# Linear attention and a low-rank mixer on one core: other zero products around q's transposes, the 1e-6 of the denominators added by PE, and v's first transfers moved between two casts

## The chip, the core and the metric

The kernel runs on one core of a Trainium2 chip. Its time is device time in microseconds. It is measured in several runs, and one further execution is recorded by the hardware profiler; that one gives the profile and the trace. The engines are named as in the profile: PE (matrix products; PEld is its weight load), DVE, ACT, POOL, and SP, which here only issues transfers. POOL issues transfers as well. All transfers are carried by the core's 16 DMA engines.

## What is computed

The reference works on q, k and v of 8 batches, 8 heads, 576 positions and 64 features, in fp32:

```python
c, s = cos(pi/2 * pos/576), sin(pi/2 * pos/576)
phi = lambda x: concat([relu(x) * c, relu(x) * s])       # 128 features
kv  = einsum('bhsf,bhsd->bhfd', phi(k), v)
den = einsum('bhsf,bhf->bhs', phi(q), phi(k).sum(2)) + 1e-6
x   = einsum('bhsf,bhfd->bhsd', phi(q), kv) / den        # heads side by side: 576 x 512 a batch
u   = x + (x.T @ U @ V).T                                # U: 576 x 32, V: 32 x 576
out = u + relu(u @ w1) @ w2                              # w1: 512 x 2048, w2: 2048 x 512
```

## The kernel before

**Tiling.** The 576 positions of a batch are cut into nines: row m of a tile holds positions of the nine m // 2, even rows the first five and odd rows the last four, so that a batch is four tiles of 128 rows (c = 0 to 3) and a tail of 64 rows (c = 4). Each of q, k and v has one staging tile (`qst`, `kst`, `vst`), which is filled by a load of the odd rows (`load_odd`, L94) and one of the even rows (`load_even`, L88). SP issues these loads in the order of the program, and a load for the next batch can only be issued when the staging tile's old content has been used.

**Order.** The schedule is written by hand: each engine executes its instructions in the order in which the program issues them. The program has an opening for batch 0 (L1176 to L1231), which is what the change touches, and then a list of slots, one group of PE products after another, with smaller work hung in between (`beside`, `todo`). In the slots, `g1_main` (L562) multiplies a 128-column piece j of w1 with the transposed u of a batch into a PSUM bank (`g_ps`, L572), and ACT applies the Relu and copies it into `hid` (L581). There are three such banks. In the first 16 slots (batch 0) hangs the attention of batch 1: its q features and transposes, then `k_prep` in slots 6, 7, 9, 10 and 12, one half on DVE (L304) and one on ACT (L302), starting with the tail `k_tl`.

**The opening.** A tile of zeros, `zero`, is made first by DVE (L140). SP issues the loads of q, of k and of the second half of v (heads 4 to 7); POOL issues the loads of V and U (`load_uv`, L165), fills constants, casts V to bf16 in three pieces (`cast_v`, L246), and only then issues the loads of v's first half (heads 0 to 3) into a tile `v0` of its own (`load_v0`, L155, issues at L156 and L160). These convert fp32 to bf16 on the way. Then POOL issues the first two quarters of w1 (`w1_load`, L115) and casts U.

PE meanwhile multiplies zeros with zeros into an unused bank (`keep_warm`, L225): `n` products of 512 columns and then `short` products of 128. Such products change no result. Then, for each c, ACT and DVE make q's features (`q_prep`) and PE transposes them, eight products of 128 columns each (`qtr_mm`, L371), with one long zero product after each group. Five copies out of PSUM (`qtr_evac`, L378: c = 0, 2, 4 by DVE, 1 and 3 by ACT) and four more long zero products follow. After that `spread_v` (L263) copies V onto all rows, and for each c the features of k are made (`k_prep`), their sums z taken (L1203), and k times v0 is summed in `kv0_mm` (L1098, the products at L1101): for c = 0 to 2 ahead of z's last round, and for the rest after it.

**first_chain** (L1113) casts the second half of v, copies z and kv out of PSUM, and computes the denominators of four heads at a time: `den_mm` (L1053) makes 20 products of one column each into a bank `d_ps`, `recip` (L407) adds 1e-6 on DVE into SBUF (L408) and takes the reciprocal there (L409). The numerators are multiplied by it (`xh_norm` by DVE, `xh_scale` by ACT), and the chain goes on to u, its transposes and the first products with w1 (L589). After `first_chain`, SP's loads of batch 1 (q, k, v) stand in the program; POOL issues the last two quarters of w1 once k's tail of batch 0 has been read (L1216), and w2 once k of batch 1 has landed (L1227).

Of the kernel before, what the change touches and what calls it, by code (L numbers as in the profile page):

```python
# [11 lines left out]
BF16 = mybir.dt.bfloat16  # L12
# [5 lines left out]
def kernel(  # L18
# [11 lines left out]
    nc = tc.nc  # L30
# [3 lines left out]
    S = 576  # L34
    D = 64
    E = D + 1
    P = 128
# [3 lines left out]
    NJ = DH // P  # L41
    NPAIR = B // 2
    TS = 64

    def tail(b):
        lo = TS * (b % 2)  # L50
# [3 lines left out]
    pool = ctx.enter_context(tc.tile_pool(name="work", bufs=2))  # L54
# [29 lines left out]
    def nines(src, b):  # L84
        return src[b].rearrange("h (m k) d -> m h (k d)", k=9)
# [41 lines left out]
    def cast(eng, o, i):  # L127
        if eng is nc.scalar:
            nc.scalar.activation(out=o, in_=i, func=AF.Copy, bias=0.0, scale=1.0)
        else:  # L130
            eng.tensor_copy(out=o, in_=i)  # L131


    V_, A_, G_ = nc.vector, nc.scalar, nc.gpsimd
# [20 lines left out]
    def load_v0():  # L155
        nc.gpsimd.dma_start(  # L156
            out=v0[1:P:2, :, 0:4].rearrange("m h c d -> m h (c d)"),
            in_=nines(v, 0)[:, 0:4, 5 * D : 9 * D],
        )
        nc.gpsimd.dma_start(  # L160
            out=v0[0:P:2].rearrange("m h c d -> m h (c d)"),
            in_=nines(v, 0)[:, 0:4, 0 : 5 * D],
        )

    def load_uv():  # L165
# [16 lines left out]
        out=iota[:, 0:4], pattern=[[2, 4]], base=0, channel_multiplier=9,  # L182
        allow_small_or_imprecise_dtypes=True,
    )
    for lo in (0, TS):
        nc.gpsimd.iota(
            out=iota[lo : lo + TS, 4:5], pattern=[[1, 1]], base=8, channel_multiplier=18,
# [3 lines left out]
        out=iota[:, 5:6], pattern=[[1, 1]], base=8, channel_multiplier=9,  # L191
# [6 lines left out]
        out=par, in_=ident[:, 1:P:2], op=ALU.add, axis=mybir.AxisListType.X  # L198
    )
    V_.tensor_scalar(  # L200
        out=iota[:, 0:4], in0=iota[:, 0:4], scalar1=par, scalar2=None, op0=ALU.add
# [19 lines left out]
    V_.memset(v_ext[:, 0:4, :, D:E], 1.0)  # L221
    V_.memset(q_tlT, 0.0)
    V_.memset(x_tl, 0.0)

    def keep_warm(n, tag, bufs, short=0):  # L225
        w_ps = ps.tile([P, 512], FP32, tag=tag, bufs=bufs, name="w_ps")
        for i in range(n + short):
            w = 512 if i < n else P
            nc.tensor.matmul(  # L229
                out=w_ps[:, 0:w], lhsT=zero[:, 0:P], rhs=zero[:, 0:w], start=True, stop=True  # L230
            )
# [6 lines left out]
    V_nat = pool.tile([R, S], BF16, tag="S2", bufs=2, name="V_nat")  # L238
# [4 lines left out]
        G_.memset(v_ext[:, 4 + i, :, :], 0.0)  # L243
        G_.memset(v_ext[tail(i), 4 + i, :, D:E], 1.0)

    def cast_v():  # L246
        nine_v = stV.rearrange("r (m k) -> r k m", k=9)
        for i in range(2):
            cast(
                G_,  # L250
                V_nat[:, 0:512].rearrange("r (c m i) -> r c m i", c=4, i=2)[:, :, :, i],
                nine_v[:, 5 * i : 5 * i + 4, :],
            )
        cast(G_, V_nat[:, 512:S], nine_v[:, 4, :])

    def cast_u():
        cast(G_, U_bf[:, 0:4, :], stU[:, 0:4, :])
# [14 lines left out]
    def spread_evac(eng):  # L272
        cast(eng, V_bf, v_ps[0].rearrange("r (c p) -> r c p", c=4))
        cast(eng, V_tl, v_ps[1][:, 0:TS])
# [5 lines left out]
    def v_prep(b, h0=0, h1=H, cs=range(5), engs=None):  # L280
        vx = v_ext
        for n, c in enumerate(cs):
            eng = engs[n] if engs else G_
            if eng is None:
                continue
            if c < 4:
                cast(eng, vx[:, c, h0:h1, 0:D], vst[:, h0:h1, c, :])
            elif b < 2:
                cast(eng, v_tl[:, h0:h1, 0:D], vst[:, h0:h1, 4, :])
            else:  # L290
                cast(eng, vx[tail(b), 4 + b % 2, h0:h1, 0:D], vst[tail(b), h0:h1, 4, :])

    def v_block(b, h0, h1, c0, c1, eng):
        cast(
            eng,
            v_ext[:, c0:c1, h0:h1, 0:D].rearrange("p c h d -> p h c d"),
            vst[:, h0:h1, c0:c1, :],
        )
# [98 lines left out]
    def qT_of(b, c, h):  # L397
        return q_pT[b][:, c, h, :] if c < 4 else q_tlT[:, h, :]
# [8 lines left out]
    def recip(rec, den):  # L407
        nc.vector.tensor_scalar(out=rec, in0=den, scalar1=1e-6, scalar2=None, op0=ALU.add)  # L408
        nc.vector.reciprocal(out=rec, in_=rec)  # L409
# [25 lines left out]
    def A_of(b):  # L435
        return A_sb[b % 4]
# [614 lines left out]
    O2, G3 = ("o", 2), ("g", 3)  # L1051

    def den_mm(b, h0, h1, d_ps):  # L1053
        for c in range(5):
            for h in range(h0, h1):
                nc.tensor.matmul(
                    out=d_ps[:, c, h - h0 : h - h0 + 1],
                    lhsT=qT_of(b, c, h),
                    rhs=z_sb[:, h : h + 1],
                    start=True,  # L1060
                    stop=True,
                )

    def xh_mm(b, c, h0, tag=None, bufs=None, acc=None):
# [41 lines left out]
    def xh_scale(b, c, h0, rec, acc):  # L1106
        for i in range(4):
            nc.scalar.activation(
                out=x_of(b, c)[:, (h0 + i) * D : (h0 + i + 1) * D], in_=acc[:, i, :],
                func=AF.Copy, bias=0.0, scale=rec[:, c, i : i + 1],  # L1110
            )

    def first_chain(b):  # L1113
        v_block(b, 4, 8, 3, 4, A_)
        v_prep(b, 4, 8, (4,), (A_,))
        v_block(b, 4, 8, 0, 3, V_)
        cast(A_, z_sb, z_ps)
        cast(V_, kv_sb[b][:, 0:4, 0:D], kv_lo)
        spread_evac(A_)
        d0 = ps.tile([P, 2, 512], FP32, tag="X", bufs=1, name="d_ps")  # L1120
        d = [d0[:, i, 0:20].rearrange("p (c h) -> p c h", h=4) for i in range(2)]
        rec = [pool.tile([P, 5, 4], FP32, tag="rec5", bufs=2, name="rec5") for _ in (0, 1)]
        den_mm(b, 0, 4, d[0])
        recip(rec[0], d[0])
        x0 = [xh_mm(b, c, 0, *G3) for c in ORD[0:3]]
        for n in (0, 1):
            xh_norm(b, ORD[n], 0, rec[0], x0[n])
        kv_unit(b, 1, *O2, A_, D)
        for c, tg in zip(ORD[3:], (O2, T1)):
            x0.append(xh_mm(b, c, 0, *tg))  # L1130
        den_mm(b, 4, 8, d[1])
        xh_scale(b, ORD[3], 0, rec[0], x0[3])
        xh_norm(b, ORD[2], 0, rec[0], x0[2])
        recip(rec[1], d[1])
        xh_norm(b, ORD[4], 0, rec[0], x0[4])
        x1 = [xh_mm(b, c, 4, *G3) for c in ORD[0:2]]
        a_ps = ps.tile([P, DM], FP32, tag="o", bufs=2, name="a_ps")
        for _ in range(2):
            nc.tensor.matmul(out=a_ps, lhsT=zero[:, 0:P], rhs=zero, start=True, stop=True)
        x1.append(xh_mm(b, ORD[2], 4, *G3))  # L1140
        x34 = ps.tile([P, 2, 512], FP32, tag="X", bufs=1, name="x34_ps")
        for i in range(2):
            x1.append(x34[:, i, 0:256].rearrange("p (i d) -> p i d", d=D))
            xh_mm(b, ORD[3 + i], 4, acc=x1[-1])
        A_mm(b, a_ps, (0, 1))
        xh_scale(b, ORD[2], 4, rec[1], x1[2])
        for n in (0, 1):
            xh_norm(b, ORD[n], 4, rec[1], x1[n])
        cast(V_, A_of(b)[0:TS, :], a_ps[0:TS, 0:P])
        uT_alloc(b)  # L1150
        for i, (tag, bufs) in enumerate((T1, O2)):
            uT_ps[b, i] = ps.tile([P, 4, P], FP32, tag=tag, bufs=bufs, name="uT_ps")
            open_mm(b, i, uT_ps[b, i], range(4))
        for i in range(2):
            uTd_mm(b, i)
        uTd_evac(b, 0, A_)
        for n in (3, 4):
            xh_norm(b, ORD[n], 4, rec[1], x1[n])
        uTd_evac(b, 1, V_)
        A_mm(b, a_ps, (2, 3))  # L1160
        cast(A_, A_of(b)[TS:P, :], a_ps[TS:P, 0:P])
        u2 = ps.tile([P, 2, 512], FP32, tag="X", bufs=1, name="u2")
        uT_ps[b, 2] = u2[:, 0, :].rearrange("p (c t) -> p c t", c=4)
        uT_ps[b, 3] = ps.tile([P, 4, P], FP32, tag="T", bufs=1, name="uT_ps")
        for i in (2, 3):
            open_mm(b, i, uT_ps[b, i], range(4))
        for i in (2, 3):
            uTd_mm(b, i)
        uTd_evac(b, 2, V_)
        uTd_evac(b, 3, A_)  # L1170
        for d in range(2):
            g_half(b, d, range(3))
        for d in range(2):
            g_half(b, d, (3,), O2)

    FEATS = [(V_, V_ if c == 3 else A_) for c in TL]  # L1176
    qT_alloc(0)
    keep_warm(4, "X", 1, 72)
    t_q = []
    for c in TL:  # L1180
        tg = G3 if c < 3 else O2
# [1 line left out]
    for c in TL:  # L1183
        q_prep(0, c, FEATS[c])
        qtr_mm(0, c, 0, H, t_q[c])
        keep_warm(1, "X", 1)
    for c, eng in zip(TL, (V_, A_, V_, A_, V_)):
        qtr_evac(0, c, eng, t_q[c])
    keep_warm(4, "X", 1)
    cast_v()  # L1190
    load_v0()
    for n in range(2):
        w1_load(n)
    cast_u()
# [5 lines left out]
    for c in TL:  # L1200
        k_prep(0, c, FEATS[c])
        for h in range(H):
            nc.tensor.matmul(  # L1203
                out=z_ps[:, h : h + 1], lhsT=k_of(0, c, h), rhs=v_tl[:, 0, D:E],
                start=(c == 0 and h == 0), stop=(c == 4 and h == H - 1),
            )
        if c < 4:
            nc.tensor.matmul(
                out=z_all[:, 1, :], lhsT=zero[:, 0:P], rhs=zero, start=True, stop=True
# [276 lines left out]
```

## Time and profile before

| what | value |
| --- | --- |
| time, median of 3 runs (lowest to highest) | 295.85 us (295.07 to 295.89) |
| time of the profiled execution | 295.75 us |
| its span, first to last instruction | 294.0 us |
| PE busy, share of the span | 288.3 us, 98% |
| DVE, ACT, POOL busy | 205.7, 161.7, 51.0 us |
| chain that ended last: PE; DMA | 89%; 6% |
| moved by the DMA engines | 54.07 MB |
| of it by SP's queue (q1); by POOL's (q0) | 43.85 MB; 9.63 MB |

The profile page lists busy time by engine, then 40 slices of the span, the DMA queues, the chain of work that ended last, the costliest groups of instructions, and the transfers with the median time from issue to landing. A time at which a transfer landed is its issue, as the timeline has it, plus that duration. Ends of products are modelled: the time that a product takes of PE is better read from the distance between two starts. The profile's column for the granted clock shows 1.00 in every window, the first microseconds included; the pace of PE is therefore read from the starts as well.

### The profile page before, as it was taken

How to read it: one execution, taken by the hardware profiler on the slowest of the kernel's cores; microseconds unless marked ns; L12 is line 12 of the kernel's file. 1: busy time of each engine (PE TensorE's matmuls, PEld its weight loads, DVE VectorE, ACT ScalarE, POOL GpSimd, SP SyncE). 2: the span in 40 equal slices, each digit the busy share in tenths (PEclk: the TensorE clock that was granted, in tenths of full speed). 3: DMA queues.
4: the chain of work that ended last, by engine and by line, in shares of the span. 5: the costliest groups of instructions: out<-in, count | busy, mean ns of one | idle time of the engine just before them, and what ended most of it. 6: DMA issues, size and time to landing. Idle time of an engine off the chain costs nothing.

```text
span 294.0 us, 7234 instructions
## 1 busy us (share of the span) xinstructions
PE 288.3 (98%) x2922; PEld 194.9 (66%) x2922; DVE 205.7 (70%) x497; ACT 161.7 (55%) x323; POOL 51.0 (17%) x89
## 2 busy tenths in 40 slices
PE   8999999999999999999999999999999999999995
PEld 6775454445745545676757666766776668889984
DVE  4878645696774569837736794678747798785864
ACT  2856654066791767568735865378752334446220
POOL 8520400012020002310500231021200100000240
PEclk9999999999999999999999999999999999999999
DMA  7999999999997998999599939992900141101013
GB/s 218 297 254 252 242 188 221 217 308 211 330 197 101 280 283 221 216 320 308 136 189 222 308 101 236 224 353 65 240 13 3 74 89 74 71 2 71 2 72 145
DMA packets 90709, 54.07 MB, mean 184 GB/s; under 512 B 58420, under 2 KB 87380, under 8 KB 90676
## 3 DMA queue, kind: packets, MB, share of 16 engines
q1 hardware_dynamic: 84116, 43.85, 59.7%
q0 software_dynamic: 6416, 9.63, 14.6%
q8 instruction: 23, 0.38, 0.5%
q10 hardware_dynamic: 144, 0.13, 0.1%
q14 instruction: 10, 0.08, 0.1%
HBM read 36.86 MB, written 9.44 MB: 157 GB/s over the span
## 4 chain that ended last, share of the span: by engine, by line
PE 89%; DMA 6%; ACT 2%; DVE 1%; issue 1%; DVEq 0%; ACTq 0%
PE g_ps L572 30%; PE h_ps L873 27%; PE o_ps L744 10%; DMA kst<-in_k_dram 6%; PE gt_ps L706 5%; PE c_ps L666 4%; PE kv_ps L343 3%; PE w_ps L229 3%; PE x_ps L418 3%; PE h_ps L744 1%; PE a_ps L441 1%; ACT k_p L302 1%; PE va_ps L471 1%; PE t_ps L373 1%; PE x_ps L1266 0%
## 5 line engine op out<-in xcount | busy, mean ns | idle before, releaser
L572 PE MATMUL g_ps<-uT,w_bf 128*128 128x512 bf16 x440 | 107.5, 379 | 0.1
L581 ACT ACTIVATE hid<-g_ps 128x512 bf16<-128x512 f32 x112 | 66.2, 599 | 72.3 <-PE g_ps L572 72.1
L572 PEld LDWEIGHTS <-w_bf 128*128 128x128 bf16 x440 | 41.3, 98 | 37.3 <-issue 0.8
L873 PEld LDWEIGHTS <-hid 128*128 128x128 bf16 x480 | 45.4, 98 | 9.6
L873 PE MATMUL h_ps<-w_bf,hid 128*128 128x256 bf16 x288 | 37.0, 273 | 0.0
L831 DVE TENSOR_TENSOR o_sb<-u_bf,h_ps 128x256 f32<-128x256 bf16 x44 | 18.3, 415 | 18.1 <-PE h_ps L873 17.9
L744 PE MATMUL o_ps<-w_bf,hid 128*128 128x512 bf16 x128 | 30.1, 379 | 0.0
L131 POOL CAST v_ext<-vst 128x512 bf16<-128x512 f32 (+1 forms) x26 | 18.5, 734 | 54.8 <-DMA vst<-in_v_dram 53.6
L873 PE MATMUL h_ps<-w_s,S 128*128 128x256 bf16 x208 | 26.5, 272 | 0.0
L873 PE MATMUL h_ps<-w_s,hid 128*128 128x256 bf16 x192 | 24.9, 273 | 0.0
L931 POOL DMA_DIRECT2D out_dram<-o_sb x16 | 10.0, 625 | 84.2 <-DVE o_sb L831 81.4
L479 DVE TENSOR_TENSOR u_bf<-x_bf,va_ps 128x512 bf16<-128x512 bf16 x27 | 17.7, 680 | 7.7 <-PE va_ps L471 5.4
L873 PEld LDWEIGHTS <-S 128*128 128x128 bf16 x208 | 19.9, 98 | 4.4
L831 DVE TENSOR_TENSOR o_sb<-o_sb,h_ps 128x256 f32<-128x256 f32 (+1 forms) x36 | 15.4, 430 | 10.4 <-PE h_ps L873 10.2
L744 PEld LDWEIGHTS <-hid 128*128 128x128 bf16 x128 | 11.6, 98 | 12.5
L706 PE MATMUL gt_ps<-uT_tl,w_bf 128*128 128x128 bf16 x256 | 16.1, 219 | 0.0
L428 DVE TENSOR_TENSOR x_bf<-x_ps,rec 128x512 bf16<-128x512 f32 x22 | 15.2, 691 | 0.8
L706 PEld LDWEIGHTS <-w_bf 128*128 128x128 bf16 x256 | 15.0, 98 | 1.0
L302 ACT ACTIVATE k_p<-kst,cosw 128x512 bf16<-128x512 f32 x20 | 14.2, 712 | 0.1
L302 ACT ACTIVATE q_p<-qst,sinw 128x512 bf16<-128x512 f32 x18 | 12.6, 709 | 1.9 <-DMA qst<-in_q_dram 1.9
L604 DVE TENSOR_TENSOR hid<-kept,c_ps 128x256 bf16<-128x256 f32 x24 | 9.4, 417 | 5.3 <-PE c_ps L666 2.8
L229 PE MATMUL w_ps<-zero 128*128 128x128 bf16 (+1 forms) x86 | 11.2, 301 | 1.2 <-DVE zero L140 1.2
(186 smaller groups left out, 419.5 us busy)
## 6 DMA issues: line engine op xcount, KB each, us to landing
qst<-in_q_dram SPq DMA_DIRECT2D x14, 512.0 KB, 6.0
kst<-in_k_dram SPq DMA_DIRECT2D x14, 512.0 KB, 6.4
vst<-in_v_dram SPq DMA_DIRECT2D x12, 512.0 KB, 6.7
out_dram<-o_sb POOLq DMA_DIRECT2D x19, 256.0 KB, 3.9
w_bf<-in_moe_w_ch_dram POOLq DMA_DIRECT2D x8, 512.0 KB, 12.3
out_dram<-o_sb SPq DMA_DIRECT2D x16, 256.0 KB, 2.8
qst<-in_q_dram SPq DMA_DIRECT2D x2, 640.0 KB, 13.6
kst<-in_k_dram SPq DMA_DIRECT2D x2, 640.0 KB, 9.0
```

What stands on the lines that cost most here:

```text
L131: eng.tensor_copy(out=o, in_=i)
L229: nc.tensor.matmul(out=w_ps[:, 0:w], lhsT=zero[:, 0:P], rhs=zero[:, 0:w], start=True, stop=True)
L302: nc.scalar.activation(out=o, in_=i, func=AF.Relu, bias=0.0, scale=w)
L428: nc.vector.tensor_tensor(out=x_of(b, c, rows).rearrange("p (g i d) -> p g i d", g=2, d=D), in0=view[:, :, :, 0:D], in1=rec[rows].unsqueez ...
L479: nc.vector.tensor_tensor(out=u_bf[b][:, j, :, :], in0=x_bf[b][:, :, ns], in1=va[b][j].rearrange("p (c n) -> p c n", c=4), op=ALU.add,)
L572: nc.tensor.matmul(out=g_ps.rearrange("p (c t) -> p c t", c=4), lhsT=w1_bf[:, d, j * P : j * P + P], rhs=uT[b][:, d, :, :], start=(d == 0) ...
L581: nc.scalar.activation(out=hid[b][:, j, :], in_=g_ps, func=AF.Relu, bias=0.0, scale=1.0)
L666: nc.tensor.matmul(out=w[to].rearrange("p (c t) -> p c t", c=2), lhsT=lhs[:, d, cs], rhs=rhs[:, d], start=(first and d == 0), stop=(d == 1 ...
L706: nc.tensor.matmul(out=g_ps[:, jj, :], lhsT=w1_bf[:, d, j * P : j * P + P], rhs=uT_tl[pr][:, d, :], start=(d == 0), stop=(d == 3),)
L744: nc.tensor.matmul(out=o[:, cols], lhsT=lhs[:, j, c * P : c * P + P], rhs=w2_bf[:, j, cols], start=(j == 0), stop=(j == NJ - 1),)
L831: eng.tensor_tensor(out=o, in0=x, in1=y, op=ALU.add)
L873: nc.tensor.matmul(out=acc, lhsT=lhs[:, j, :], rhs=rhs[:, j, :], start=(j == 0 and at is not None), stop=(j == 7), skip_group_check=at is ...
```

## The change

Three things are changed, all in the opening.

1. The zero products: ahead of q, 13 long and 10 short ones take the place of 4 long and 72 short ones; the long one after each group of transposes is left out; after the copies there are 8 long ones instead of 4.
2. The denominators: a tile `eps` of one row holds 128 values of 9.98e-07, 128 of 1.62e-09 (in bf16; their sum is 1e-6) and 20 ones, filled by three DVE memsets. `den_mm` first multiplies each of the two pieces with the ones, which fills the bank's 20 columns with 1e-6, and adds the 20 products to that. DVE then takes the reciprocal straight from PSUM, without the addition.
3. POOL: the casts of V are cut in two calls. The loads of v0 are issued after the first of the three casts, and the other two casts follow the loads.

```diff
+    EPS = (9.98377799987793e-07, 1.622538547962904e-09, 1.0)
...
+    eps = pool.tile([1, 2 * P + 20], BF16, tag="S2", bufs=2, name="eps")
+    for cs, part in zip((slice(0, P), slice(P, 2 * P), slice(2 * P, None)), EPS):
+        V_.memset(eps[:, cs], part)
...
-    def cast_v():
+    def cast_v(i):
         nine_v = stV.rearrange("r (m k) -> r k m", k=9)
-        for i in range(2):
-            cast(
-                G_,
-                V_nat[:, 0:512].rearrange("r (c m i) -> r c m i", c=4, i=2)[:, :, :, i],
-                nine_v[:, 5 * i : 5 * i + 4, :],
-            )
-        cast(G_, V_nat[:, 512:S], nine_v[:, 4, :])
+        cast(
+            G_,
+            V_nat[:, 0:512].rearrange("r (c m i) -> r c m i", c=4, i=2)[:, :, :, i],
+            nine_v[:, 5 * i : 5 * i + 4, :],
+        )
+        if i:
+            cast(G_, V_nat[:, 512:S], nine_v[:, 4, :])
...
     def den_mm(b, h0, h1, d_ps):
+        for i in range(2):
+            nc.tensor.matmul(
+                out=d_ps.rearrange("p c h -> p (c h)"), lhsT=eps[:, i * P : i * P + P],
+                rhs=eps[:, 2 * P :], start=(i == 0), stop=(i == 1),
+            )
         for c in range(5):
             for h in range(h0, h1):
                 nc.tensor.matmul(
...
-                    start=True,
+                    start=False,
                     stop=True,
+                    skip_group_check=True,
                 )
...
-        recip(rec[0], d[0])
+        V_.reciprocal(out=rec[0], in_=d[0])
...
-        recip(rec[1], d[1])
+        V_.reciprocal(out=rec[1], in_=d[1])
...
-    keep_warm(4, "X", 1, 72)
+    keep_warm(13, "X", 1, 10)
...
         qtr_mm(0, c, 0, H, t_q[c])
-        keep_warm(1, "X", 1)
     for c, eng in zip(TL, (V_, A_, V_, A_, V_)):
         qtr_evac(0, c, eng, t_q[c])
-    keep_warm(4, "X", 1)
-    cast_v()
+    keep_warm(8, "X", 1)
+    cast_v(0)
     load_v0()
+    cast_v(1)
```

## The prediction

> **What bounds the kernel now.** PE carries the time: page part 1 gives it 288.3 of 294.0 us, and part 4 puts 89% of the chain that ended last on it. But a busy PE is busy with the zero products too, so I read, in this order, the chain of waits for the first 42 us, the engines' timeline, and the DMA view cut into windows.
>
> The chain of waits, first 42 us (start, length, what):
>
> ```profile
> 12.50 1.88 ACT k_p L302 x3
> ...
> 15.68 17.15 DMA kst<-in_k_dram
> ...
> 32.92 0.72 ACT k_tl L302
> 33.64 0.48 ACT hid L581
> 34.12 0.61 ACT k_p L302
> 34.73 0.49 ACT hid L581
> ...
> 35.27 3.70 PE g_ps L572 x16
> ```
>
> Here the end is tied not to the opening work but to the load of batch 1's k (L88, even rows), issued at 15.68 and landed at 15.68 + 17.15 = 32.83. ACT executes in order: its k_tl waits for that load, the Relu of g1's j=7 is queued behind k_tl, and PE's j=10 needs the bank that this Relu frees. From 31.46 to 38.81 PE runs 32 products of L572 at 0.216 us (6.91 us) in 7.35 us: 0.44 us are stalls. So whatever the opening gains ends in this wait; PE could have been 0.44 us later or a good deal earlier with nearly the same end.
>
> The opening, timeline of PE (start, length, line, idle before):
>
> ```profile
> 1.19 7.92 PE L229 MATMUL w_ps<-zero 128*128 128x512 bf16 x76 [1.19 <-DVE zero L140]
> 8.94 0.61 PE L373 MATMUL t_ps<-ident,q_p 128*128 128x128 bf16 x8
> ...
> 11.59 0.61 PE L373 MATMUL t_ps<-ident,q_tl 128*128 128x128 bf16 x8
> 12.04 1.46 PE L229 MATMUL w_ps<-zero 128*128 128x512 bf16 x5
> ...
> 16.16 0.52 PE L1101 MATMUL kv_ps<-v,k_p 128*128 128x64 bf16 x12 [0.54 <-DMA v<-in_v_dram]
> ```
>
> The first transposes start only when the 76 zero products are through, and the opening's one real stall is the wait for v's first half (v0).
>
> The DMA view of 8 to 11 us, and below it of 14 to 30 us (packets, MB, share of the 16 engines' time):
>
> ```profile
> q1 hardware_dynamic: 951, 1.09, 103.1%
> q0 software_dynamic: 12, 0.00, 0.4%
> ```
>
> ```profile
> q0 software_dynamic: 1883, 1.86, 68.6%
> q1 hardware_dynamic: 1914, 2.14, 46.6%
> ```
>
> q1 holds SP's loads (q, k, second half of v, then batch 1), q0 POOL's (v0, w1). The engines are full from about 3 us on; while both queues have work they are served packet for packet.
>
> **The change, part by part.** The sum is made against the profiled execution: 295.75 us, span 294.0, so 1.75 outside it; the median of the runs is 295.85.
>
> *Zero products ahead of q.* The four long ones took 1.68 us (0.42 each), then 40 short ones 4.16 us (0.104), then 33 short ones 1.65 us (0.050): PE ran at half pace until about 7.1. Now 13 long at 0.42 end near 6.7, four short at 0.104 reach 7.1, six at 0.056 reach 7.5. q's first piece is ready when ACT's L302 (7.08, 0.72) ends at 7.8, so the transposes start there, 1.1 us sooner. Without the long product between groups, five groups of eight at 0.056 (0.45) follow the features; the last waits for DVE's q_tl (9.34 + 0.80 = 10.14) and ends near 10.6 instead of 12.04. ACT's two copies of q_pT (1.02 each) and DVE's three (0.69) follow: ACT is free for k at about 11.5 (before 12.50), DVE at 12.0 (before 12.85). But k's even rows, issued at 3.06, land 9.0 us later, at 12.1. So k_p starts near 12.25: 0.25 us sooner on ACT, 0.6 on DVE. The eight long products (8 x 0.216 = 1.73) end near 12.3, and hide there.
>
> *The transfers of v0.* POOL's timeline: three casts of V from 6.13, 1.64 us; the issues at 7.72 (0.66) and 8.37 (0.77); w1's from 9.13. With one cast (0.57 to the next start) ahead, the issues move to 6.70 and 7.36, 1.02 us sooner. The other two casts end near 9.1: w1's issues stay, and V_nat, needed at 13.43 (then about 12.4), is still in time. In the DMA view q0 moves nothing from 9.05 to 10.95 and starts in the window 10.9 to 11.4, 3.2 us after the issue; I carry this delay over, so v0 starts near 9.9. Then q1 still holds k's last rows and the second half of v (landings 12.1, 12.75 and 14.3), and these are now shared. v0's last piece landed at 8.37 + 7.7 = 16.1; it gains between 0 and 1.0, I take 0.7. kv0 then starts near 15.4 instead of 16.16.
>
> What the earlier start takes from q1 is the **term that decides**. Alone, q1 moves 951 / 3 = 317 packets per us, 20 per engine; each of those 20 is now followed by one of q0. Before, w1's last piece, issued at 16.50, landed after 18.4 us at 34.9, so on the slowest engine 2.1 us of q0's work came after batch 1's k. A pair takes 16 engines x 16 us / 1,900 = 0.135 us, so 2.1 us are 15.6 pairs: fewer than 20, so all of q0's rest moves ahead of k. q0's part of a pair is 68.6 / (68.6 + 46.6) = 0.60, and 0.60 x 2.1 = 1.26 us. k of batch 1 lands 1.26 us later, near 34.1. Bounds: 0 (v0 starts no sooner on that engine) and 1.5 (20 packets x 0.135 x 0.6 = 1.6, less the small packets of v0). That k's load is issued 0.6 us sooner (its odd rows wait for DVE's k_p, ended at 14.91) doesn't help: q of batch 1 is ahead of it in the queue until 10.21 + 13.6 = 23.8.
>
> *1e-6 by PE.* Two products of 20 columns are added before each group of 20 denominators. Those of one column start 0.025 us apart (16 in 0.40), those of 512 0.216 apart: 0.05 to 0.43 for two; I take 0.05, by the nearer row. DVE loses two adds (starts 17.84 and 19.55; 0.21 each to the reciprocal). What reading PSUM costs a reciprocal no row shows; the add from PSUM took 0.18, the reciprocal from SBUF 0.28, so -0.1 to +0.1. DVE gains 0.16 twice, but PE is without a pause from 17.17 to 20.4, and the products with U at 20.53 could move by 0.12 at most, less the 0.10 added: 0. Three memsets (0.07 to 0.09, some 0.12 apart) fall into DVE's 2.65 us idle ahead of 7.10. eps takes the one free buffer of its pair; the next user comes after 70 us.
>
> *Sum.* Opening 0.7 sooner, paid into the wait at 32.9: 0. Batch 1's k 1.26 later: +1.26, as ACT, then PE, wait for it one for one. 295.75 + 1.26 = **297.0**.
>
> **The rivals.**
>
> *No landing moves* (295.6). If v0 is held up by what q1 already has in the engines, and not by its own 3.2 us, issuing it sooner moves neither v0 nor k. For it: v0 starts just as q1's first loads run out. Against it: the first U load (issued 2.47) started near 6.0 in the middle of q1's work, 3.5 us on. The opening gains 0.25 from k_p, and the wait takes all but about 0.15. [...] The trace shows 3.2 us and can't split it.
>
> *Faster: k of batch 1 lands sooner.* The chain of waits runs through the issue at 15.68. If landing follows issue, k comes 0.6 sooner, the opening (0.7) keeps up, and the end is 295.75 - 0.6 = 295.15; with v0's whole 1.0 us and the stalls of 0.44 it could reach 294.6. It decides as soon as k lands before 32.8 and PE is there. Against it: engines full and q ahead until 23.8.
>
> *PE's pace drops.* From 7.5 to 10.6 PE now has only transposes, 2.25 of 3.1 us. If the pace halved at 10.6 for as long as it took to rise at the start (1.19 to 7.1, 5.9 us), the eight long products take 3.4 us, V's spread 0.5, the four rounds of z about 2.5 to 3.3: kv0 starts at 17.0 to 17.8, 0.9 to 1.6 later; less the 0.44 that the wait covers, the end is 296.2 to 296.9. With the forecast it doesn't add: both are waited for at the same place. Against it: PE idled 0.54 us ahead of 16.16 and kept its pace. [...]
>
> **How the numbers follow.** Forecast 0.48 (own range 296.4 to 297.4), no landing moves 0.22, faster 0.18, pace 0.12. What a measurement of this kernel can tell from no change is about 0.3%, 0.89 us: below 294.96 is faster, above 296.74 slower. Forecast: 0.38 slower, 0.10 same; no landing: 0.22 same; faster: 0.13 and 0.05 same; pace: 0.10 slower, 0.02 same. Together 0.13 faster, 0.39 same, 0.48 slower. Range 295.0 to 297.8: down to most of the faster case, up to the forecast with its upper bound and some of the pace.
>
> **What would show it.** Right: first transposes near 7.8, the last group ends near 10.6; v0 issued at 6.7 and landed near 15.4, v's second half landed after 15; batch 1's k landed near 34 and w1's last piece no longer after it; PE's stall before g1's j=10 grown to 1 us or more. Wrong: k of batch 1 at 32.8 or sooner, or 512-column products more than 0.4 us apart after 10 us.

## The result: 0.8% slower in the first set, by a stop of PE that no step foresaw

| what | before | after |
| --- | --- | --- |
| median of 6 runs, taken side by side (lowest to highest) | 295.73 us (295.07 to 297.13) | 297.94 us (297.43 to 298.95) |
| ratio, 95% interval | | 1.0078 (1.0049 to 1.0106) |
| profiled execution, its span | 295.75, 294.0 us | 298.51, 296.7 us |
| mean granted clock of PE in it | | 0.994 |

A later set of 12 runs of the same changed kernel (experiment 3) gave 296.65 us; how the two sets go together is told there. A ratio, here and below, leaves out runs that lie far above a kernel's fastest, while a median is of all runs.

The chain of waits of the changed kernel, first 45 us (start, length, what):

```profile
18.36 0.51 PE d_ps L1061 x17
18.87 1.20 issue
20.07 0.23 PE d_ps L1061 x3
...
25.48 1.83 PE g_ps L589 x8
...
33.86 6.91 PE g_ps L572 x32
```

Two things differ from before. The wait for batch 1's k is gone: 32 products of L572 now run in 6.91 us, which is 32 x 0.216. In its place stands "issue", 1.20 us in which PE waits for nothing that the profile shows, in the middle of the second group of denominators, after 17 of its 20 products. The timeline of PE says the same, and shows what follows:

```profile
15.11 0.51 PE L1107 MATMUL kv_ps<-v,k_p 128*128 128x64 bf16 x12
...
18.71 0.16 PE L1061 MATMUL d_ps<-z_sb,q_tlT 128*128 128x1 bf16 x1
20.07 0.23 PE L1061 MATMUL d_ps<-z_sb,q_tlT 128*128 128x1 bf16 x3 [1.20 <-issue]
...
22.70 1.04 PE L1099 MATMUL uT_ps<-ident,x_bf 128*128 128x128 bf16 x8
```

The first products with v0 start at 15.11 (before: 16.16), so the opening is 1 us ahead between these two executions. Behind the stop, eight products of 128 columns take 1.04 us, where eight of the same shape took 0.61 in the opening. The windows view of the changed kernel names the reason in its column PEclk, the granted clock:

```profile
core 0: us, PE busy (x) PEld busy (x) DVE busy (x) ACT busy (x) POOL busy (x), PEclk, DMA share, GB/s
16.96:20.37 3.41, 2.21 (x71) 2.04 (x68) 1.39 (x5) 1.20 (x5) 0.00 (x0) 1.00 1.17 253
20.37:23.78 3.41, 3.41 (x41) 2.35 (x37) 2.13 (x7) 0.93 (x4) 0.00 (x0) 0.50 1.16 258
```

For exactly one stretch of 3.41 us, starting 0.3 us after PE has resumed, the clock is half.

**Where the time went.** Timeline of PE, before:

```profile
19.28 0.24 PE L1056 MATMUL d_ps<-z_sb,q_tlT 128*128 128x1 bf16 x4
...
23.18 1.90 PE L589 MATMUL g_ps<-uT,w_bf 128*128 128x512 bf16 x8
...
38.81 0.44 PE L343 MATMUL kv_ps<-v_ext,k_p 128*128 128x65 bf16 x4
```

and changed:

```profile
25.41 1.90 PE L589 MATMUL g_ps<-uT,w_bf 128*128 128x512 bf16 x8
...
40.61 0.28 PE L343 MATMUL kv_ps<-v_ext,k_p 128*128 128x65 bf16 x4
```

The 18th product of that group starts at 20.07; before, it started near 19.31 (the second of the row that starts at 19.28). Without the stop it would have started at 18.74: a lead of 0.57, turned by the stop of 1.33 into 0.76 late. From there to L589's first product it takes 25.41 - 20.07 = 5.34 us, before 23.18 - 19.31 = 3.87: 1.47 for the half clock. 0.76 + 1.47 = 2.23 us late at L589. The wait for k, no longer needed, gives back 0.43: the first product of L343 behind it starts at 40.61, before at 38.81, 1.80 late. The rest of the 2.7 us came at 194 us, where two starts of PE lay 0.94 us further apart than one product takes: a wait for a transfer that turns q of batch 7 (`186.50 8.77 DMA q_pT<-q_p` in the chain). In the later profile of the same kernel only a weight load waits there, for 0.6 us.

**What PE waited for.** The DMA view has a queue that the prediction passed over, q8, of kind "instruction". Changed kernel, 17.7 to 19 us:

```profile
q8 instruction: 1, 0.02, 4.7%
```

It moves instructions in packets of 0.02 MB (16,384 bytes in the trace). Over the whole span there are 22 in the changed kernel and 23 before. PE has 2872 products and as many weight loads in the changed kernel: if all 22 are PE's, that is an estimated 5744 / 22 = 261 instructions a packet. The first packet within the span starts at 17.84 in the changed kernel; before, at 13.84. PE stopped 0.9 us after the packet's start and went on 2.2 us after it.

The length of the half-clock stretch, 3.41 us, comes back in both traces. In the changed kernel PE's pace doubles at 6.72 us (products of 128 columns start 0.056 us apart from there, 0.107 in the slow part of the kernel before), and the half clock begins 13.65 us later, at 20.37: 4 times 3.413. In the kernel before the pace doubles at 7.16 us, and the clock next falls at 293.88, behind the last product, 286.72 us later: 84 times 3.413. So the clock is granted here in windows of 3.41 us, which don't lie at the same place in every execution; their ends are counted from there below.

So the **theory** to test: the zero products also carry PE through its instructions. A packet brings PE a block of them, and it is called for when PE has come far enough in those before. The change takes 54 zero products out of the opening (85 before, 31 after), the first packet then starts 4 us later (17.84, before 13.84), and the wait for it falls into the stretch of 1-column products, which start 0.025 us apart and use a block up faster than the next one arrives; PE runs dry, and a window with such a hole in it costs the next one half its clock. **Rivals**: the clock fell because of the stretch of transposes up to 11.27 us; the reading of PSUM or the eps products stall PE; v0's transfers delay batch 1's k.

### The profile page after: what moved, and what is told of

It is laid out like the page before. It is cut to its first block, busy times and chain, and to the rows that moved or that the text cites. A ratio compares the mean times of both kernels' runs of the same rounds, so it can differ in the third digit from the quotient of the medians.

```text
span 296.7 us, 7135 instructions
## 1 busy us (share of the span) xinstructions
PE 288.7 (97%) x2872; PEld 191.8 (65%) x2872; DVE 206.8 (70%) x498; ACT 161.7 (55%) x323; POOL 53.0 (18%) x89
## 4 chain that ended last, share of the span: by engine, by line
PE 90%; DMA 5%; DVE 3%; issue 1%; SPq 0%; ACT 0%; DVEq 0%
PE g_ps L572 31%; PE h_ps L873 25%; PE o_ps L744 10%; PE gt_ps L706 5%; PE c_ps L666 4%; DMA q_pT<-q_p 3%; PE kv_ps L343 3%; PE x_ps L418 2%; DMA qst<-in_q_dram 2%; PE a_ps L441 1%; PE h_ps L744 1%; DVE q_p L304 1%; PE va_ps L471 1%; PE t_ps L361 1%; PE w_ps L229 1%
## 5 line engine op out<-in xcount | busy, mean ns | idle before, releaser
L572 PE MATMUL g_ps<-uT,w_bf 128*128 128x512 bf16 x440 | 107.1, 379 | 0.0
L572 PEld LDWEIGHTS <-w_bf 128*128 128x128 bf16 x440 | 41.3, 98 | 36.9
L128 POOL CAST v_ext<-vst 128x512 bf16<-128x512 f32 (+1 forms) x26 | 20.1, 798 | 58.3 <-DMA vst<-in_v_dram 45.8
L479 DVE TENSOR_TENSOR u_bf<-x_bf,va_ps 128x512 bf16<-128x512 bf16 x27 | 17.7, 681 | 7.7 <-PE va_ps L471 5.3
L831 DVE TENSOR_TENSOR o_sb<-o_sb,h_ps 128x256 f32<-128x256 f32 (+1 forms) x36 | 15.4, 431 | 9.9 <-PE h_ps L873 9.7
L408 DVE TENSOR_SCALAR rec<-x_ps 128x8 f32<-128x8 f32 (+2 forms) x39 | 6.3, 161 | 9.6 <-PE x_ps L418 8.2
```

The costliest lines, as they stand in the source:

```text
L479: nc.vector.tensor_tensor(out=u_bf[b][:, j, :, :], in0=x_bf[b][:, :, ns], in1=va[b][j].rearrange("p (c n) -> p c n", c=4), op=ALU.add,)
L572: nc.tensor.matmul(out=g_ps.rearrange("p (c t) -> p c t", c=4), lhsT=w1_bf[:, d, j * P : j * P + P], rhs=uT[b][:, d, :, :], start=(d == 0) ...
L831: eng.tensor_tensor(out=o, in0=x, in1=y, op=ALU.add)
```

## The experiments

A run with 3.41 us at half clock has a mean granted clock near 0.994 (1 - 0.5 x 3.41 / 296); so the mean clock, which every run has, tells which runs had such a stretch (below 0.996), and I count them as "half". Ratios are against runs of the kernel before on the same chip.

| kernel | median, us | ratio to before (95%) | half | median of the others | PE's stop |
| --- | --- | --- | --- | --- | --- |
| after, first set | 297.94 | 1.0078 (1.0049 to 1.0106) | 6 of 6 | | 1.20 |
| `after2`, the same again | 296.65 | 1.0016 (0.9986 to 1.0046) | 4 of 12 | 295.83 | 1.2 |
| `zero_only` | 296.32 | 1.0003 (0.9978 to 1.0029) | 5 of 12 | 295.70 | 1.46 |
| `long6` | 297.22 | 1.0024 (0.9987 to 1.0061) | 6 of 12 | 296.51 | 1.33 |
| `pad27` | 297.53 | 1.0034 (1.0002 to 1.0065) | 7 of 12 | 296.33 | 0.63 |
| `no_zero` | 296.19 | 1.0003 (0.9977 to 1.0028) | 1 of 12 | 296.04 | none |
| `pad54` | 295.71 | 1.0011 (0.9983 to 1.0039) | 1 of 12 | 295.69 | none |
| `v0_only` | 295.50 | 0.9983 (0.9956 to 1.0010) | 0 of 12 | 295.50 | none |
| `eps_only` | 295.82 | 0.9994 (0.9970 to 1.0018) | 2 of 12 | 295.80 | none |
| `fill6` | 296.70 | 1.0046 (1.0023 to 1.0069) | 1 of 12 | 296.68 | none |
| `w1late` | 295.81 | 1.0006 (0.9982 to 1.0030) | 1 of 12 | 295.52 | none |
| `w1half` | 297.53 | 1.0046 (1.0016 to 1.0077) | 2 of 12 | 297.29 | none |
| before, all runs beside these eleven | | | 9 of 110 | 295.80 | none |

### 1. Which part: `zero_only`, `no_zero`

`zero_only` is the kernel before with part 1 of the change alone; `no_zero` is the changed kernel with the zero products of before:

```diff
-    keep_warm(13, "X", 1, 10)
+    keep_warm(4, "X", 1, 72)
...
         qtr_mm(0, c, 0, H, t_q[c])
+        keep_warm(1, "X", 1)
...
-    keep_warm(8, "X", 1)
+    keep_warm(4, "X", 1)
```

> Only the zero products are changed; the 1e-6 and v0's transfers stay as before. Theory (fetch): PE's stop of 1.2 us in the second den_mm is PE waiting for its own instructions. With 54 fewer zero products the block that it needs next is asked for later (the instruction transfer starts at 17.84 instead of 13.84), while the one-column products use instructions up at 25 ns a product; the stop then lets the clock fall to half for 3.4 us. Here: the stop (0.8 to 1.4 us) and the half clock are both there, 297.4 to 298.4 us. Rival (eps): the one-row products of eps, or rival (v0): the earlier transfers, cause the stop; then no stop here and 295.3 to 296.0 us.

> The changed kernel with the zero products of before; the 1e-6 by PE and the earlier transfers of v0 stay. Fetch: no stop, no half clock, the instruction transfer back near 14 us; 295.2 to 295.9 us. Rivals eps and v0: the stop remains, above 297.0 us.

The stop is there with the zero products alone and gone without them. Timeline of PE in `zero_only`:

```profile
17.66 0.24 PE L1056 MATMUL d_ps<-z_sb,q_tlT 128*128 128x1 bf16 x4
17.75 0.19 PE L1068 MATMUL xh_ps<-kv,q_tlT 128*128 128x64 bf16 x1
19.40 0.27 PE L1068 MATMUL xh_ps<-kv,q_tlT 128*128 128x64 bf16 x3 [1.46 <-issue]
```

The place tells most. `zero_only` has no eps products, so four PE products fewer ahead of this point, and it stops four products later: after all 20 denominators and one more, where the changed kernel stopped after 17. The stop keeps its number in PE's instructions, not its line. In time, though, `zero_only` missed the 297.4 us that were expected at least, and is 1.0003 of before: 297.11 us in the five runs with the half clock, 295.70 in the other seven. The profiled execution kept its full clock in spite of the stop (its own time, 297.21, has two waits of 0.6 and 0.7 us much further on), so the stop alone is not enough. `no_zero` came out at 296.19, a little above the 295.2 to 295.9 that were expected, and can't be told from before (1.0003).

### 2. Number or activity: `long6`, `pad54`, `pad27`

`long6` adds six long zero products, more activity with few instructions; `pad54` and `pad27` add 54 or 27 zero products of one column, instructions with next to no activity:

```diff
-    keep_warm(13, "X", 1, 10)
+    keep_warm(19, "X", 1, 10)          # long6
+    keep_warm(13, "X", 1, 10, 54)      # pad54: 54 products of one column; pad27: 27
```

> The changed kernel with 6 more long zero products ahead of q (19 long, 10 short): 1.3 us more activity, but only 12 more instructions. Fetch: the stop remains, 0.8 us or more, 297.3 to 298.5 us. Rival (activity): PE stops or cools because too little work was given to it; then the clock stays full and the time is 295.5 to 296.2 us.

> The changed kernel with 54 zero products of one column after the 10 short ones: as many instructions as before ahead of the chain, but only about 1.4 us of PE, most of it in the wait for q. Fetch: the block is asked for some 100 instructions earlier, no stop, no half clock, 295.0 to 296.0 us. Rival (activity): hardly any activity is added, so the stop and the half clock remain, above 297.0 us.

> The changed kernel with 27 one-column zero products after the 10 short ones, half of what took the stop away. Fetch: the instruction transfer starts near 16 us instead of 17.8, PE runs dry earlier in the program (in the products of kv for heads 4 to 7 or just behind) and for 0.3 to 0.9 us; 295.7 to 297.0 us, some of the runs at a clock of 0.994. Rival (activity): 27 products of one column change nothing, the stop stays at 1.2 us in the second den_mm.

`long6` kept the stop, and 6 of 12 runs kept the half clock. The chain of waits of `long6`:

```profile
19.45 0.36 PE d_ps L1061 x11
19.82 1.33 issue
21.15 0.38 PE d_ps L1061 x9
```

Six more products ahead, and the stop comes after 11 of the 20 instead of 17: six sooner. In `pad27` it comes 27 sooner, at the last product with the second half of v (18.05), the clock was half from 20.01, and 7 of 12 runs were half. The profile puts 0.63 us of this stop down to ACT, but in the timeline of the weight loads the next one waits for nothing that the profile shows:

```profile
18.87 0.30 PEld L1074 LDWEIGHTS <-q_pT 128*128 128x128 bf16 x8 [0.75 <-issue]
```

With 54, the first instruction packet starts at 12.49 us, as early as in the kernels with the old zero products (12.7 to 13.8), no stop is left, and 1 run of 12 was half. The place of each stop came as expected; of the medians, that of `pad54` did, that of `long6` (297.22) fell just short of 297.3, and that of `pad27` (297.53) lay above 297.0.

The traces say it to the instruction. Counted by weight loads, one to each product, the stop comes behind the 219th in all five profiles that have it, and the 220th follows 2.2 to 2.4 us after the start of the first instruction packet. In the eight profiles without a stop, PE comes to its 219th only 2.7 to 5.5 us after that start. So the number of PE's instructions decides over the stop, and activity doesn't. That rules out the rival with the transposes too: `pad54` has the same transposes without long products between them, and no lowered clock behind them in its profile (mean 1.000).

### 3. The same kernel again, and the other parts alone: `after2`, `v0_only`, `eps_only`

`after2` is the changed kernel unaltered; `v0_only` and `eps_only` are the kernel before with part 3 or part 2 alone.

> The changed kernel once more, unaltered. Theory (fetch and clock): the stop in the second den_mm is in every execution, but the clock halves only in those in which one of its windows of 3.41 us, which run freely, holds the whole stop. So two groups: mean granted clock 0.994 at 297.4 us and more, and full clock at 295.7 to 296.5 us. Rival (stop alone): all runs are at 297.4 us or more, whatever their clock.

> The kernel before with v0's two transfers issued between the casts of V, and nothing else. Prediction on record: k of batch 1 lands near 34 us instead of 32.8, 296.7 to 297.3 us. Rival, after the profiles so far (k of batch 1 at 32.4 to 33.2 us with and without the earlier transfers): no landing moves by more than it differs between executions, no stop, 295.4 to 296.4 us, the same as before.

> The kernel before with the 1e-6 by PE, and nothing else. Fetch: 8 more instructions ahead of the stop's place, so no stop; PE pays about 0.2 us for each pair of one-row products (gaps of 0.10 and 0.07 us around them in the changed kernel), DVE saves two additions; all of it covered by the wait for k of batch 1: 295.4 to 296.4 us. Rival (eps): the one-row products or the reciprocal from PSUM hold up the chain beyond that cover, above 296.6 us.

`after2` has the stop at the same product (18.30 to 19.6 us), but only 4 of its 12 runs are half: 298.5 us against 295.83 in the other eight. So the same kernel has the half clock in some runs and not in others, 10 of 18 together. Whether the first set's 6 of 6 was bad luck is not shown: if the two sets are alike, chance puts all of the first six among the 10 about once in 90 times. What was expected for `after2`, that the clock halves when one window of 3.41 us holds the whole stop, fits the five profiles with a stop: it lies within one window in the four with a half clock (which begins 0.30 us after PE has resumed in the changed kernel, 0.38 in `after2`, 0.95 in `long6` and 1.14 in `pad27`, so at no fixed distance), and in `zero_only`, which kept its clock, a window ends at 18.20, inside the stop of 17.94 to 19.40. Five profiles don't show it. Taken together, kernels with the stop were half in 28 of 54 runs, those without it in 8 of 84, before in 9 of 110.

The other two parts cost nothing. `eps_only` is 0.9994 and has no stop; each pair of eps products adds 0.23 us to PE, as was expected (from the long product ahead of the first group to its first denominator 16.07 to 16.52, before 16.95 to 17.17), and the reciprocal takes 0.28 from PSUM, as it did from SBUF. `v0_only` is 0.9983, and batch 1's k didn't come later by it.

### 4. Filling the hole: `fill6`

```diff
+        for _ in range(6):
+            nc.tensor.matmul(
+                out=d0[:, 1, 20:512], lhsT=zero[:, 0:P], rhs=zero[:, 20:512], start=True, stop=True
+            )
         den_mm(b, 4, 8, d[1])
```

> The kernel after the change, with six zero products of 492 columns (0.205 us each, 1.23 in all, written into unused columns of the same bank) ahead of the second group of denominators, so that PE has work for most of the time in which it otherwise stands still from 18.7 to 20.1 us. Theory (the stop comes from PE's own instructions, which arrive at about 20.0 whatever PE does meanwhile; and it is the stop's share of a 3.41 us window that halves the clock behind it): PE's idle time before 20.1 shrinks from 1.2 us to at most 0.5, the product groups behind it start at the same time as without the six, and fewer than one run in four shows the half clock: median 295.7 to 296.4. Rival (a late second group of denominators costs by itself, or zero products do not count towards the clock): six runs in ten or more still show it, median 297 or more. Third case: with six more products the instructions run out 12 places sooner and the stop stays just as long behind them: then the end comes 1 us later than theory, 297.0 to 297.5.

The hole is gone from the profile and the half clock from the runs (1 of 12, against 10 of 18 in the changed kernel without the six). Timeline of PE in `fill6`:

```profile
19.02 1.41 PE L1138 MATMUL d_ps<-zero 128*128 128x492 bf16 x6
20.36 0.20 PE L1055 MATMUL d_ps<-eps 1*128 1x20 bf16 x2
```

The price was missed: 296.68 without the half clock, where 295.7 to 296.4 was expected. In the profiled execution v's second half landed at 16.25 instead of 14.55 and PE had waited 0.7 us for it; the six started that much later and came on top. Whether this was so in all 12 runs isn't seen. What the run shows is the second half of the theory: with products in place of the hole the clock stays up (in 11 of 12 runs).

### 5. What holds the lead back: `w1late`, `w1half`

Without a stop, the 1 us that the opening gains should show in the end, but `pad54` is 295.69. It waits for batch 1's k as the kernel before did; chain of waits of `pad54`:

```profile
14.77 17.58 DMA kst<-in_k_dram
...
32.44 0.72 ACT k_tl L302
```

`w1late` is `pad54` with the last quarter of w1 issued behind this k; `w1half` moves only the half of the quarter that is needed later:

```diff
     G_.tensor_copy(out=mark, in_=k_tl[0:TS, 7, 0:1])
-    for n in range(2, 4):
-        w1_load(n)
+    w1_load(2)                  # w1half: also w1_load(3, 0, 256)
...
     G_.tensor_copy(out=mark, in_=kst[0:TS, 7, 4, 0:1])
+    w1_load(3)                  # w1half: w1_load(3, 256, 512)
```

> The kernel after the change, with 54 zero products of one column put back (so that PE does not run out of instructions) and the last quarter of w1 issued only after batch 1's k has landed, ahead of w2, instead of before it. Theory (the opening now has a lead of 1 us, and the end does not show it because the wait for batch 1's k, at 32.4 us whatever v0's transfers do, takes it; k shares the DMA engines with w1's last quarter): k's even rows land 0.8 to 1.5 us sooner, by 31.6, the wait at 33 us goes, and the time is 294.7 to 295.4. Rival (something else takes the lead, or w1's last quarter, which g1's j=12 needs near 35.7 us, is now what comes late): k lands sooner but PE waits for w1 or ACT instead, 295.7 or more; if w1's quarter lands at 37 or later, 297 or more.

> The kernel after the change with the 54 one-column zero products put back, and the last quarter of w1 cut in two: the columns of j = 12 and 13 issued where the quarter was issued, those of j = 14 and 15 after batch 1's k has landed. Theory (only the wait for batch 1's k, and behind it that for w1, keeps the opening's lead of 1 us from the end): k's even rows land between the 30.0 us of the run with the whole quarter late and the 32.4 of the run with none late, near 31.2; w1's second half lands before 36; neither is waited for by more than 0.2 us; the columns' j = 15 starts 0.6 to 0.9 us sooner than in the kernel before (39.57) and the time is 294.8 to 295.3. Rival (a wait further on, or the spread from run to run, takes the lead): j = 15 sooner by as much, but the time stays at 295.5 to 296.0. Second rival (half a quarter is still too late or k is): a gap of 0.4 us or more on PE between 31 and 37, time 295.5 or more.

Chain of waits of `w1late`:

```profile
14.81 15.20 DMA kst<-in_k_dram
...
30.59 5.37 DMA w_bf<-in_moe_w_ch_dram
```

k lands at 30.01, 2.3 us sooner than in `pad54`, and isn't waited for any more: it does share the DMA engines with w1, and 0.5 MB out of its way was worth that much between these two executions. But now w1's last quarter, landed at 35.96, is late for j = 12. The rival was right, and the lead still doesn't reach the end. `w1half` fell short in a third way: k landed at 32.2, hardly sooner than in `pad54` (32.35), and w2's first quarter, behind the rest in POOL's queue, was late for the first products with w2. `w1half`, waits of PE (what waits, for whom, us in total, times, longest):

```profile
PE o_ps L744 <- DMA w_bf<-in_moe_w_ch_dram: 1.3, 1, 1.3
```

No version was found that beats the kernel before beyond what the measurement can tell. The loads of batch 1, w1 and w2 set the pace up to 42 us (k, landed at 32.35, in `pad54`, w1's last quarter at 35.96 in `w1late`, w2's first at 41.81 in `w1half`), and none of these versions carries the opening's lead to the end.

## Why the prediction was wrong

It said slower, 297.0, and slower it was, 297.94 in the first set; but not for its reason.

**The step that failed** is the term that decides: v0's transfers start 1 us sooner, and their work ahead of batch 1's k makes k land 1.26 us later, at 34.1. Neither half holds. The issues did move to 6.70 and 7.35, as worked out. But the start of the transfers moved by some 0.2 us: in the DMA view of 10.4 to 10.9 us q0 has nothing in the kernel before, and in the changed kernel, and in `v0_only`,

```profile
q0 software_dynamic: 10, 0.01, 7.4%
```

```profile
q0 software_dynamic: 7, 0.00, 5.2%
```

where a start near 9.9, about 1 us sooner, had been forecast. The 3.2 us between issue and start were not a delay of v0's own: in the changed kernel, from 6.70 to 10.74, they are 4.0. It starts at 10.7 to 11.0 whether it was issued at 6.70 or at 7.72. What it waits for is not shown: q1's share falls there from 102% of the engines (9.05 to 10.95 us, before) to 80% (10.9 to 11.4), which can be the cause, or what q0 takes. This is the rival "no landing moves", whose place the trace of before could not tell from the forecast's.

And k landed at 32.48, sooner than before and not later. POOL's copy that waits for it, in the changed kernel:

```profile
32.60 0.18 POOL L1233 COPY mark<-kst 64x1 f32<-64x1 f32 x1 [15.81 <-DMA kst<-in_k_dram]
```

Where v0 is issued sooner and w1 as before (after, `after2`, `v0_only`, `no_zero`, `long6`, `pad54`, `pad27`, `fill6`), k landed at 31.5 to 33.3, mean 32.55; where it isn't (before, `zero_only`, `eps_only`), at 32.4 to 32.8, mean 32.54. The bounds of the term, 0 to 1.5, were real, and its lower end was true. The 2.1 us that w1 had left behind k were of one execution. Time to landing of w1's third and fourth quarters, from the DMA view, in the kernel before and in `eps_only`, which leaves v0 where it was:

```profile
w_bf<-in_moe_w_ch_dram POOLq DMA_DIRECT2D x2, 512.0 KB, 16.8
```

```profile
w_bf<-in_moe_w_ch_dram POOLq DMA_DIRECT2D x2, 512.0 KB, 13.7
```

In `eps_only` all of w1 has landed (32.23) ahead of k (32.41), the case that was to cost 1.26, and k isn't late.

**What no step had** is the count of instructions. The zero products were costed by their time alone. The cover that they gave is the very thing that the prediction was to name: with 85 of them the first instruction packet starts at 12.7 to 13.8 us and PE doesn't stop; with 31 it starts at 17.84 in the changed kernel, and the price is a stop of 1.2 to 1.5 us. The stop by itself cost next to nothing in two kernels, as the opening's lead and the wait for k cover it (295.83 in the runs of `after2` without the half clock and 295.70 in those of `zero_only`, 295.80 before); in `long6` and `pad27` these runs lie at 296.51 and 296.33, and why isn't shown. What costs most is the window at half clock behind it: 1.4 us between the medians of the half runs and the others in `zero_only`, 1.8 in `pad27`, 2.3 in `long6`, 2.7 in `after2`.

**Point by point.** *First transposes* 7.8: 8.30, because q landed later in that execution (ACT's first features at 7.53, not 7.08). *Last group ends* 10.6: it starts at 10.82 and the long products follow at 11.27; the distance of the groups was right. *k's features* 12.25 on ACT, 12.0 to 12.4 on DVE: 11.92 and 12.39. *kv0* 15.4: 15.11. *v0 landed* 15.4: 14.94. The opening gained 1.05 at kv0, 0.7 had been taken; but how much of that is the change's isn't shown, since v0 landed at 13.47 in `eps_only` and at 13.89 in `zero_only`, where it is issued behind all three casts, and kv0 started at 15.29 in `eps_only`, whose opening is that of the kernel before. *The eps products* 0.05 a pair: 0.23, within the bounds given (0.05 to 0.43); the nearer row was the wrong one to take. *The zero products* at half pace start 0.107 and 0.427 apart, not 0.104 and 0.42, which changes nothing. *The reciprocal* within 0.1: no change, 0.28. *PE's pace drops* came true in its effect, 3.41 us at half clock, but behind the stop and 10 us later; the stretch from 7.5 to 10.6, which it feared, kept its clock. That the forecast's direction came true is luck: the term that should have made the kernel slower came to nothing, and something else did. *What would make it wrong* was said rightly: "k of batch 1 at 32.8 or sooner".

**What stays open.** What starts an instruction packet is not in the trace, nor is any engine's name on it; that q8's first packet is PE's rests on the stop's fixed place in PE's count and on PE's going on 2.2 to 2.4 us after the packet's start in all five profiles with a stop. The packet doesn't start at a fixed count: PE stands at its 124th to 133rd weight load then in the kernels with the old zero products or `pad54`'s, and at its 167th to 196th in the others. An estimate that fits: 3 us before the start, PE stands at its 91st to 113th in all 13 profiles, so the call may go out there. Why a window with a hole of 1.2 us halves the clock in half the runs and not in the others was not settled: PE's busy share does not tell it, 2.21 of 3.41 us in the window that did it in the changed kernel and 2.16 from 18.20 to 21.61 us in `zero_only`, which kept its clock. Nor does a hole within one window: while it waits for q, `fill6` stands still for 1.21 us up to 7.99, in a window that is as idle as the one at issue, and the next has its full clock. Windows view of `fill6`:

```profile
5.38:8.79 3.41, 2.20 (x26) 1.48 (x25) 1.56 (x3) 1.58 (x3) 3.29 (x8) 1.00 0.99 343
8.79:12.20 3.41, 3.00 (x37) 2.12 (x36) 3.41 (x7) 2.91 (x4) 2.69 (x6) 1.00 1.16 332
```

Most products around that hole are long ones, around the stop they have 1 to 64 columns; whether this makes the difference was not tested.

## What to carry to other kernels

Instructions that do nothing for the result can still count by their number (here a stop of 1.2 us came when 54 zero products went, and was gone with 54 of one column put back): before taking out zero products, count how many instructions lie ahead of the next stretch of tiny products (here the stop came behind the 219th weight load), and look at the instruction queue's packets beside PE's timeline. A stop of 1 us that seems covered can cost about twice its length through the clock (1.4 to 2.7 us here), so look at the granted clock in the windows behind it, and at several executions, since it comes in some only. And a landing time read from one execution, with queues full, is good to a microsecond or more (batch 1's k landed at 31.5 to 33.3 us in eight profiles): a forecast must not rest on which of two transfers was last in it.

## What the runs showed of the hardware

- The instruction queue q8 moved packets of 16,384 bytes, 22 of them in the changed kernel's span; if all are PE's, that is one for an estimated 261 instructions. Among products of 1 to 64 columns (20 denominators in 0.5 us, 20 products with 64 columns in 0.59), PE stood still 0.6 to 1.5 us in five profiles, always behind its 219th weight load (17 of 20 in the changed kernel; 6 sooner with 6 more ahead, 27 sooner with 27 more, 4 later with 4 fewer), and went on 2.2 to 2.4 us after the start of q8's first packet. That it had used up its instructions there is a reading of these numbers.
- Behind a hole of 0.6 to 1.5 us among products of 1 to 64 columns, the granted clock was half for the 3.41 us of the next window in four of five profiles. The mean clock was below 0.996 in 28 of 54 runs of kernels with this hole, against 17 of 194 without; a hole of 1.21 us behind long products (`fill6`, up to 7.99) left the clock full. The window before the half clock was busy 2.21 of 3.41 us in the changed kernel and 2.79 of 3.42 in `pad27`.
- The two products of one row and 20 columns (the eps products) cost PE 0.23 us a pair, where products of one column start 0.025 us apart.
